# One PSUM tile of two banks and one addition for both column halves of the second product; two banks for the convolution

## The chip, the cores and the metric

The kernel runs on one core of a Trainium2 chip. The metric is the device time of one launch in microseconds. Five engines work side by side, each through its own list of instructions in order: TensorE (PE in the profile) multiplies matrices into PSUM, VectorE (DVE) and ScalarE (ACT) read PSUM and write SBUF, GpSimd (POOL) works on SBUF, and SyncE (SP) issues transfers. PSUM has eight banks; one bank holds 128 rows of 512 float32 numbers, and one product of this kernel is gathered in one bank.

## What is computed

Two branches share the normalised input, and their sum is added to the input:

```python
x = A_q                                   # (1, 2048, 576)
xn = _layernorm(x, axis=-1)
# branch A: short causal convolution of k (4 taps), times v, a long causal convolution
# of each of the 576 channels (length 2048), plus kv * ssm_D, times xn
kv = k_shift * v
y = irfft(rfft(kv_pad) * rfft(ssm_k_pad))[:S] + kv * ssm_D
# branch B: 576 -> 4608, relu, 4608 -> 576
h = jnp.maximum(jnp.einsum("bsd,df->bsf", xn, w1), 0)
return x + xn * y + jnp.einsum("bsf,fd->bsd", h, w2)
```

## The kernel before

**Precision.** Each float32 operand is split into a high and a low part, and a product is the sum of high times high, high times low and low times high. So every product is three matmuls per 128 rows of the contraction.

**Branch B, the products.** The 2048 rows are 16 tiles of 128 (t), in four blocks of four tiles (b); two blocks make a half, and the halves are worked through one after the other. The 4608 hidden columns come in 12 chunks of 384 per half (ci runs from 0 to 23), each of three tiles of 128 columns (j). `mm1` (L304) computes one hidden tile of 128 by 512 with 14 matmuls of 512 columns into one bank of the pool `ps_h` (two banks); ScalarE takes the relu into `hh` (L319) and VectorE the rest into `ll` (L320). `mm2` (L323) multiplies them with the second weights: for each row tile t and each of two halves h of the 576 output columns, nine matmuls of 288 columns (L334) into one bank of the pool `ps_o` (three banks), and then VectorE adds the bank, times the row's 1/std, to the accumulator `acc[t]` in SBUF (L337). That is 2 x 16 x 12 = 384 groups of nine matmuls and 384 additions of 128 by 288.

**Branch A, the convolution.** A generator, `conv` (L379), makes it in four stages, each a Fourier step written as matrix products of 288 columns into banks of the pool `ps_f` (three banks, `fft_psum`, L134):
- fk: 64 tiles of the kernel's transform, two matmuls each (L369), read by ScalarE (L370); VectorE splits the operands (L363).
- fx: 64 tiles of the data's transform, again L369 and L370. Here VectorE also computes the four taps (L454, L457, L458), the gate (L463) and the split (L363).
- fm: 32 groups of six tiles, three matmuls each (L533). Two tiles of k are read four times each by ScalarE (L556 to L559), two of x are read twice by ScalarE (L583, L584) and once by VectorE (L585), two of the result once by ScalarE (L573). VectorE also has L524, L563, L566 and L587.
- fo: 32 units, two for each row tile t, of two tiles, two matmuls each (L657, L658). ScalarE moves half of a tile (`low`, L659) and VectorE adds the other half to it (L660). VectorE splits the operands of a unit (`olo`, L618, after ScalarE's `ohi`, L617), multiplies the finished row tile by the gate (L625) and adds it to the accumulator, or to what the first half of the rows had stored (L632). Its loads (`zo`, `xt`, `ft`) are on SP's queue, its matrices (`wi`) and its stores for t below 8 on POOL's.

Stage four cannot start before the last group of stage three has been stored, since its loads take all of them.

**What sets the order.** The program is written with the two branches woven: after each half of an `mm1` and each half of an `mm2`, `tick` (L685) lets the generator take as many steps as its share of the work allows. When the products of the second half of the rows are in their last chunk, `rest_of_stream` (L680) writes down all that is left of the convolution ahead of the store of the row tile. This written order gives priorities only. A scheduler of the compiler then makes the list of each engine on a timeline of its own: an instruction takes its place when its operands, and a free buffer of its pool, are there by that timeline. So a pool's number of banks changes the lists of all engines. `done["acc"]` holds the last addition; the convolution's work on VectorE and ScalarE is held behind it (`here`, L373).

```python
    ps_h = ctx.enter_context(tc.tile_pool(name="ps_h", bufs=2, space=PSUM))
    ps_o = ctx.enter_context(tc.tile_pool(name="ps_o", bufs=3, space=PSUM))
    ps_f = ctx.enter_context(tc.tile_pool(name="ps_f", bufs=3, space=PSUM))
```

Of the kernel before, what the change touches and what calls it, by code (L numbers as in the profile page):

```python
# [10 lines left out]
F32 = mybir.dt.float32  # L11
F32R = mybir.dt.float32r
AF = mybir.ActivationFunctionType
OP = mybir.AluOpType
PSUM = bass.MemoryType.PSUM
DRAM = bass.MemoryType.DRAM

P = 128
# [5 lines left out]
NH = D // 2  # L24
# [83 lines left out]
def h3_ffn_kernel(ctx: ExitStack, tc, x, k, v, shift_k, ssm_k, ssm_D, w1, w2, fwd, inv, mid, out):  # L108
    nc = tc.nc
# [8 lines left out]
    xp = ctx.enter_context(tc.tile_pool(name="xp", bufs=2))  # L118
    dram = ctx.enter_context(tc.tile_pool(name="dram", bufs=1, space=DRAM))
    ps_h = ctx.enter_context(tc.tile_pool(name="ps_h", bufs=2, space=PSUM))  # L120
    ps_o = ctx.enter_context(tc.tile_pool(name="ps_o", bufs=3, space=PSUM))
    ps_f = ctx.enter_context(tc.tile_pool(name="ps_f", bufs=3, space=PSUM))

    ident = const.tile([P, P], F32, name="ident")
    make_identity(nc, ident)
# [1 line left out]
    rstd = const.tile([P, T], F32, name="rstd")  # L127
# [6 lines left out]
    def fft_psum():  # L134
        return ps_f.tile([P, 512], F32, tag="f", name="psf")

    def two(t):

        return t.rearrange("p (h n) -> p h n", h=2)


    acc = {}
# [5 lines left out]
    def move(tile_, rows, t, store=False, queues=(nc.sync, nc.sync)):  # L148
        for u in range(U):
            a, b = tile_[halves(u)[0]], rows[u, :, t]  # L150
            queues[u].dma_start(*((b, a) if store else (a, b)))
# [12 lines left out]
    def stats(t, src):  # L164
        st = xp.tile([P, 2, 6], F32, tag="bn", name=f"bn{t}", bufs=4)
        for h in range(2):
            nc.vector.bn_stats(st[:, h, :], src[:, h * NH:(h + 1) * NH])
        nc.vector.bn_aggr(mv[:, t, :], st)

    def inv_std(t0, n):  # L170

        q = xp.tile([P, 3, BT], F32, tag="q", name=f"q{t0}")[:, :, :n]
        va, h0, qu = q[:, 0, :], q[:, 1, :], q[:, 2, :]
        nc.vector.tensor_scalar(va, mv[:, t0:t0 + n, 1], EPS, None, op0=OP.add)
        nc.scalar.activation(h0, va, AF.Sqrt, scale=0.25)
        nc.vector.reciprocal(qu, h0)
        nc.vector.tensor_tensor(qu, va, qu, OP.mult)
        nc.vector.scalar_tensor_tensor(qu, qu, 0.25, h0, op0=OP.mult, op1=OP.add)
        nc.vector.reciprocal(rstd[:, t0:t0 + n], qu)
# [5 lines left out]
    def centred(dst, src, t):  # L185


        return nc.vector.tensor_scalar(dst, src, mv[:, t, 0:1], None, op0=OP.subtract)

    xT = {}  # L190
    done = {}

    def xT_tiles(b):
        hi = xp.tile([P, 4, 512], F32R, tag="xhi", name=f"xhi{b}")
        lo = xp.tile([P, 4, 512], F32R, tag="xlo", name=f"xlo{b}")
        hl = xp.tile([P, 512], F32R, tag="xhl", name=f"xhl{b}")
        xT[b] = (hi, lo, hl)

    def split_x(b, c, ps):
        hi, lo, hl = xT[b]  # L200
        if c < 4:
            nc.scalar.activation(hi[:, c, :], ps, AF.Copy)
            nc.vector.tensor_tensor(lo[:, c, :], ps, hi[:, c, :], OP.subtract)  # L203
        else:
            done["act"] = nc.scalar.activation(hl[:64, :], ps[:64, :], AF.Copy)
            done["dve"] = nc.vector.tensor_tensor(hl[64:, :], ps[:64, :], hl[:64, :],
                                                  OP.subtract)

    def first_xT(srcs):

        xT_tiles(0)
        ps = []
        for c in range(5):
            ps.append(ps_o.tile([P, 512], F32, tag="o", name=f"psx{c}") if c >= 3 else fft_psum())
        neg = xp.tile([P, BT], F32, tag="neg", name="neg", bufs=1)
        behind = None
        for t in range(BT):
            if t % 2 == 0:
                pair = xp.tile([P, 2, D], F32, tag="xn", name=f"xn{t}", bufs=BT // 2)
            xn = pair[:, t % 2, :]  # L220
            with tc.issue_after(behind.ins) if behind else nullcontext():
                stats(t, srcs[t])
                if t % 2 == 0:
                    behind = nc.vector.tensor_scalar(neg[:, t:t + 1], mv[:, t, 0:1], -1.0, None,
                                                     op0=OP.mult)
                    nc.scalar.activation(xn, srcs[t], AF.Identity, bias=neg[:, t:t + 1])
                else:
                    behind = centred(xn, srcs[t], t)
            for c in range(5):
                w = min(P, D - c * P)  # L230
                nc.tensor.transpose(ps[c][:w, t * P:(t + 1) * P], xn[:, c * P:c * P + w], ident)
        for c in range(5):
            split_x(0, c, ps[c])
        with tc.issue_after(done["dve"].ins):
            inv_std(0, BT)
# [87 lines left out]
    def mm2(ci, b, i):  # L323
        t = b * BT + i
        cols = slice(i * P, (i + 1) * P)
        for h in range(2):
            ps = ps_o.tile([P, 512], F32, tag="o", name=f"pso{ci}_{t}_{h}")
            dc = slice(h * NH, (h + 1) * NH)
            n = 0
            for j in range(FT):  # L330
                hh, ll = hid[ci, b, j]
                _, _, h2, l2 = weights[ci][j]
                for a, m in ((hh, h2), (hh, l2), (ll, h2)):
                    nc.tensor.matmul(ps[:, :NH], a[:, cols], m[:, dc],  # L334
                                     start=n == 0, stop=n == 3 * FT - 1)
                    n += 1
            done["acc"] = nc.vector.scalar_tensor_tensor(  # L337
                acc[t][:, dc], ps[:, :NH], rstd[:, t:t + 1], acc[t][:, dc],
                op0=OP.mult, op1=OP.add)
            tick(W_MM2 / 2)  # L340
        if ci % NCHUNK == NCHUNK - 1:
            if t >= HT:
                rest_of_stream()
            if t < HT:
                if t % 2:
                    nc.sync.dma_start(fin[t // 2], pairs[t - 1])
            else:
                if t >= T - 2:
                    move(acc[t], out, t, store=True)
                elif t % 2:  # L350
                    move(pairs[t - 1], out, slice(t - 1, t + 1), store=True)
# [328 lines left out]
    def rest_of_stream():  # L680
        for _ in stream:
            pass
        clock["done"] = True

    def tick(cost):  # L685

        if clock["done"] or clock["ffn"] < clock["until"]:
            clock["ffn"] += cost
            return
        clock["ffn"] += cost  # L690
        clock["conv"] += rate * cost
        if clock["conv"] < 0:
            return
        try:
            c = next(stream)
        except StopIteration:
            clock["done"] = True
            return
        if c < 0:
            clock["until"] = clock["ffn"] - c  # L700
        else:
            clock["conv"] -= c
# [11 lines left out]
    for i in range(N_WARM):  # L714
        nc.tensor.matmul(idle, warm[:, :P], warm, start=True, stop=True)
    split_w1(0, 0)
    first_xT(acc)
    for j in range(1, FT):
        split_w1(0, j)
# [9 lines left out]
    def drain(n):  # L729
        nonlocal prev  # L730
        if prev is None:
            return
        ci, b, done = prev
        for _ in range(n):
            if done < BT:
                mm2(ci, b, done)
                done += 1
        prev = (ci, b, done) if done < BT else None

    for half in range(HALVES):  # L740
        for cc in range(NCHUNK):
            ci = half * NCHUNK + cc
# [56 lines left out]
```

## Time and profile before

| | |
|---|---|
| median of three runs | 1118.28 us (1117.45 to 1119.73) |
| the profiled execution, its own time | 1114.96 us |
| span of that execution, first to last instruction | 1113.2 us |
| mean granted TensorE clock | 0.989 of full speed |
| busy share: PE, DVE, ACT, POOL | 97%, 66%, 52%, 24% |
| fk, fx, fm, fo: first to last matmul start (us) | 121 to 223, 258 to 462, 480 to 965, 983 to 1084 |

Times in the profile are microseconds from the first instruction of the span. PE is the matmul, PEld the load of its weights, which overlaps it; matmuls overlap each other too, so that their durations add up to more than the time they take. A row of a group names line, engine, operation, output and inputs, shape, count; behind the bar stand the busy time in us, the mean duration in ns, and the idle time of the engine ahead of these instructions with what ended most of it. A row of waits names who waited for whom, the sum in us, the number and the longest.

### The profile page before, as it was taken

The numbers are of one execution on the slowest core, as the hardware profiler recorded it, in microseconds if no ns is written. First come the engines' busy times: TensorE is split into PE (matmuls) and PEld (weight loads), VectorE is DVE, ScalarE is ACT, GpSimd is POOL, SyncE is SP. The second block draws the span as 40 slices with busy tenths as digits, with TensorE's granted clock in tenths as the row PEclk, the third lists the DMA queues.
The fourth block names the chain that finished last, engine by engine and source line by source line (L and its number), as shares of the span: only waits on it lengthen the run. The fifth ranks groups of instructions, "written<-read, shape, count | busy, mean of one in ns | idle before, by whom it ended". The sixth has DMA issues, their size and how long they took to land.

```text
span 1113.2 us, 17349 instructions
## 1 busy us (share of the span) xinstructions
PE 1080.5 (97%) x6534; PEld 980.5 (88%) x6534; DVE 737.3 (66%) x1215; ACT 583.5 (52%) x1180; POOL 265.4 (24%) x215
## 2 busy tenths in 40 slices
PE   8999999999999999999999999999999999998698
PEld 5889999988898988999989999999999999997587
DVE  6353876759999999358555654655555655468985
ACT  4221778713433343357566665676656666545540
POOL 3230331412412313303121131220312302214200
PEclk9999999999999999999999999999999999999699
DMA  9940464664544533426544133342342412288823
GB/s 236 175 144 1 145 192 138 191 184 140 178 145 152 180 118 130 142 75 201 175 132 132 54 122 99 96 121 64 121 123 63 131 54 90 89 247 248 232 73 86
DMA packets 112640, 150.79 MB, mean 135 GB/s; under 512 B 45229, under 2 KB 63279, under 8 KB 112556
## 3 DMA queue, kind: packets, MB, share of 16 engines
q1 hardware_dynamic: 104572, 135.98, 41.2%
q0 software_dynamic: 7824, 13.11, 4.5%
q8 instruction: 51, 0.84, 0.3%
q10 hardware_dynamic: 160, 0.59, 0.2%
q14 instruction: 33, 0.27, 0.1%
HBM read 114.26 MB, written 35.39 MB: 134 GB/s over the span
## 4 chain that ended last, share of the span: by engine, by line
PE 69%; DVE 16%; DMA 6%; issue 4%; ACT 3%; SPq 1%; POOL 1%; DVEq 0%; ACTq 0%; POOLq 0%
PE pso L334 30%; PE psh L314 29%; PE psf L533 6%; DVE e L457 4%; DVE acc L337 3%; DVE c L458 3%; DMA r<-in_w 2%; PE psf L369 2%; DVE ll L320 1%; DVE xs L363 1%; DVE c L454 1%; SPq L392 1%; DVE c L463 1%; DMA k-1_2411<-in_k 1%; POOL l L262 1%
## 5 line engine op out<-in xcount | busy, mean ns | idle before, releaser
L262 POOL TENSOR_TENSOR l<-r,h 128x640 fp32r<-128x640 f32 (+1 forms) x144 | 229.5, 1609 | 646.6 <-ACT h L297 318.7
L334 PE MATMUL pso<-h,hh 128*128 128x288 f32 x1152 | 339.0, 296 | 7.9 <-DVE acc L337 7.6
L334 PE MATMUL pso<-l,hh 128*128 128x288 f32 x1152 | 339.2, 295 | 0.0
L334 PE MATMUL pso<-h,ll 128*128 128x288 f32 x1152 | 338.9, 295 | 0.0
L337 DVE SCALAR_TENSOR_TENSOR acc<-pso,rstd,acc 128x288 f32<-128x288 f32 x384 | 193.4, 512 | 90.1 <-PE pso L334 88.3
L334 PEld LDWEIGHTS pso<-h,hh 128*128 128x128 f32 x1152 | 216.3, 188 | 17.4 <-DVE acc L337 11.3
L314 PE MATMUL psh<-xhi,h 128*128 128x512 f32 x576 | 226.7, 394 | 1.5 <-DVE ll L320 1.1
L314 PE MATMUL psh<-xlo,h 128*128 128x512 f32 x576 | 226.2, 393 | 0.0
L314 PE MATMUL psh<-xhi,l 128*128 128x512 f32 x576 | 225.6, 392 | 0.0
L334 PEld LDWEIGHTS pso<-l,hh 128*128 128x128 f32 x1152 | 216.8, 188 | 5.3
L334 PEld LDWEIGHTS pso<-h,ll 128*128 128x128 f32 x1152 | 216.7, 188 | 0.7
L320 DVE SCALAR_TENSOR_TENSOR ll<-psh,hh 128x512 fp32r<-128x512 f32 x144 | 98.6, 686 | 123.2 <-ACT hh L319 122.9
L319 ACT ACTIVATE hh<-psh 128x512 fp32r<-128x512 f32 x144 | 85.1, 593 | 141.4 <-PE psh L314 139.8
L314 PEld LDWEIGHTS psh<-xhi,l 128*128 128x128 f32 x576 | 108.5, 188 | 21.7
L314 PEld LDWEIGHTS psh<-xhi,h 128*128 128x128 f32 x576 | 108.3, 188 | 18.4 <-DVE ll L320 1.6
L314 PEld LDWEIGHTS psh<-xlo,h 128*128 128x128 f32 x576 | 108.5, 188 | 15.9 <-DVE xlo L203 0.4
L289 ACT ACTIVATE h<-r 128x640 fp32r<-128x640 f32 x72 | 52.4, 734 | 62.8 <-PE psh L314 30.4
L297 ACT ACTIVATE h<-r 128x576 fp32r<-128x576 f32 x72 | 46.9, 678 | 52.7 <-DMA r<-in_w 29.1
L585 DVE TENSOR_TENSOR k<-psf,k 128x288 f32<-128x288 f32 x64 | 29.1, 455 | 66.8 <-ACT sw L584 66.6
L583 ACT ACTIVATE sw<-psf 64x288 f32<-64x288 f32 x64 | 26.1, 408 | 88.9 <-PE psf L533 87.7
L314 PE MATMUL psh<-xhl,l 128*128 128x512 f32 x144 | 56.5, 392 | 0.0
L314 PE MATMUL psh<-xhl,h 128*128 128x512 f32 x144 | 56.2, 391 | 0.0
(104 smaller groups left out, 1414.3 us busy)
## 6 DMA issues: line engine op xcount, KB each, us to landing
r<-in_w SPq DMA_DIRECT2D x24, 864.0 KB, 6.6
r<-in_w SPq DMA_DIRECT2D x23, 768.0 KB, 5.6
zk<-zk SPq DMA_DIRECT2D x32, 288.0 KB, 2.4
zx<-zx SPq DMA_DIRECT2D x32, 288.0 KB, 2.4
ztk<-zk SPq DMA_DIRECT2D x32, 288.0 KB, 2.8
ztx<-zx SPq DMA_DIRECT2D x32, 288.0 KB, 2.8
zy<-vo SPq DMA_DIRECT2D x32, 288.0 KB, 2.2
zo<-zy SPq DMA_DIRECT2D x32, 288.0 KB, 3.5
```

The lines of the kernel that those rows point to most:

```text
L262: return nc.gpsimd.tensor_tensor(dst, src, hi, OP.subtract)
L289: nc.scalar.activation(h1, r1[:, :, cols], AF.Copy)
L297: nc.scalar.activation(h2, r2[:, j, :], AF.Copy)
L314: nc.tensor.matmul(ps, a, m, start=i == 0, stop=i == len(seq) - 1)
L319: done["act"] = nc.scalar.activation(hh, ps, AF.Relu)
L320: nc.vector.scalar_tensor_tensor(ll, ps, 0.0, hh, op0=OP.max, op1=OP.subtract)
L334: nc.tensor.matmul(ps[:, :NH], a[:, cols], m[:, dc], start=n == 0, stop=n == 3 * FT - 1)
L337: done["acc"] = nc.vector.scalar_tensor_tensor(acc[t][:, dc], ps[:, :NH], rstd[:, t:t + 1], acc[t][:, dc], op0=OP.mult, op1=OP.add)
L457: nc.vector.tensor_tensor(e, win[t - n], sk[:, n, :], OP.mult)
L458: nc.vector.tensor_tensor(sums[t], sums[t], e, OP.add)
L533: nc.tensor.matmul(ps[:, :NH], a, m[:, cols], start=n == 0, stop=n == 2)
L585: nc.vector.tensor_tensor(k1[:, cols], ps, k1[:, cols], OP.mult)
```

## The change

Both halves of the output columns of a row tile go into one tile of two banks, and VectorE adds both in one operation of 128 by 576. The pool `ps_o` has two such tiles, four banks in place of three, and `ps_f` gives one up, two in place of three. The first transposes of the input, which borrow banks from both pools, are dealt out accordingly.

```diff
-    ps_o = ctx.enter_context(tc.tile_pool(name="ps_o", bufs=3, space=PSUM))
-    ps_f = ctx.enter_context(tc.tile_pool(name="ps_f", bufs=3, space=PSUM))
+    ps_o = ctx.enter_context(tc.tile_pool(name="ps_o", bufs=2, space=PSUM))
+    ps_f = ctx.enter_context(tc.tile_pool(name="ps_f", bufs=2, space=PSUM))
...
-            ps.append(ps_o.tile([P, 512], F32, tag="o", name=f"psx{c}") if c >= 3 else fft_psum())
+            if c < 2:
+                ps.append(fft_psum())
+            else:
+                if c % 2 == 0:
+                    two_banks = ps_o.tile([P, 2, 512], F32, tag="o", name=f"psx{c}")
+                ps.append(two_banks[:, c % 2, :])
...
+        ps = ps_o.tile([P, 2, 512], F32, tag="o", name=f"pso{ci}_{t}")
         for h in range(2):
-            ps = ps_o.tile([P, 512], F32, tag="o", name=f"pso{ci}_{t}_{h}")
...
-                    nc.tensor.matmul(ps[:, :NH], a[:, cols], m[:, dc],
+                    nc.tensor.matmul(ps[:, h, :NH], a[:, cols], m[:, dc],
                                      start=n == 0, stop=n == 3 * FT - 1)
                     n += 1
-            done["acc"] = nc.vector.scalar_tensor_tensor(
-                acc[t][:, dc], ps[:, :NH], rstd[:, t:t + 1], acc[t][:, dc],
-                op0=OP.mult, op1=OP.add)
+            if h == 1:
+                done["acc"] = nc.vector.scalar_tensor_tensor(
+                    two(acc[t]), ps[:, :, :NH], rstd[:, t:t + 1], two(acc[t]),
+                    op0=OP.mult, op1=OP.add)
```

In the changed kernel the lines from `mm2` on have numbers higher by five or six: L657 is L663 there, and the addition L337 is L343.

## The prediction

> **What bounds the kernel now.** I read the page first (engines, slices, chain), then the windows by stage, then the waits in each, then the timeline of the last stage. In the windows the columns are stretch, length, busy time with instructions in brackets per engine, granted clock, DMA share, GB/s.
>
> ```profile
> span 1113.2 us, 17349 instructions
> ...
> PE 1080.5 (97%) x6534; PEld 980.5 (88%) x6534; DVE 737.3 (66%) x1215; ACT 583.5 (52%) x1180; POOL 265.4 (24%) x215
> ```
>
> ```profile
> core 0: us, PE busy (x) PEld busy (x) DVE busy (x) ACT busy (x) POOL busy (x), PEclk, DMA share, GB/s
> 258.30:461.70 203.40, 198.76 (x1205) 180.57 (x1204) 181.92 (x251) 75.69 (x148) 53.34 (x42) 1.00 0.45 139
> 479.80:964.50 484.70, 484.00 (x3012) 446.56 (x3011) 276.54 (x481) 313.41 (x673) 97.10 (x62) 1.00 0.35 107
> 983.00:1086.00 103.00, 87.86 (x485) 76.85 (x484) 91.44 (x157) 52.12 (x109) 21.91 (x33) 0.90 0.67 198
> ```
>
> The stretches are the convolution's stages two (fx), three (fm) and four (fo), by the first and last matmul of each. In fm TensorE is full (484.0 of 484.7) and VectorE has 43% free: shortening evictions there buys nothing. In fx and above all in fo VectorE is nearly full (182 of 203, 91 of 103) and TensorE waits. Two limits, then: TensorE's total of work, and VectorE in two stages. The rows of first and last starts follow (ks is stage one, fk). Since the last stage's results must precede the last products, when fo starts and how long it takes sets the end.
>
> ```profile
> L369 PE MATMUL psf<-ks,wk x128: 290/294/372, 121.0 to 222.9; 128*128 128x288 f32 x128
> L369 PEld LDWEIGHTS psf<-xs,wx x128: 187/188/191, 258.3 to 461.7; 128*128 128x128 f32 x128
> ...
> L657 PE MATMUL psf<-ohi,wi x64: 288/299/609, 983.1 to 1084.3; 128*128 128x288 f32 x64
> ...
> L658 PE MATMUL psf<-olo,wi x64: 288/294/445, 983.2 to 1084.4; 128*128 128x288 f32 x64
> ```
>
> Matmuls overlap, so their pitch, not their duration, is their cost. The chain in order of time has it:
>
> ```profile
> 84.48 3.57 PE pso L334 x27
> ...
> 94.84 3.20 PE psh L314 x14
> ...
> 1049.15 3.62 PE pso L334 x18
> ```
>
> 3.57/27 = 0.132 us for 288 columns, 3.20/14 = 0.229 us for 512. All matmuls of the program at these pitches (0.085 for a transpose, an estimate below the 288-column one) come to 1056.4 us; I call a sum of this kind TensorE work.
>
> **The change, part by part.** *The merged eviction.* 384 additions become 192 twice as wide.
>
> ```profile
> L337 DVE SCALAR_TENSOR_TENSOR acc<-pso,rstd,acc 128x288 f32<-128x288 f32 x384 | 193.4, 512 | 90.1 <-PE pso L334 88.3
> ...
> L320 DVE SCALAR_TENSOR_TENSOR ll<-psh,hh 128x512 fp32r<-128x512 f32 x144 | 98.6, 686 | 123.2 <-ACT hh L319 122.9
> ...
> L632 DVE SCALAR_TENSOR_TENSOR acc<-y,rstd,acc 128x576 f32<-128x576 f32 x8 | 6.5, 813 | 0.2
> ```
>
> The nearest row is L632: the same operation with the same scalar and accumulator on 576 columns, from SBUF, 0.813 us. Bounds: 0.74 (0.686 plus 64 columns at the same slope) and 1.02 (twice 0.512, nothing saved). I take 0.813: 193.4 - 192 x 0.813 = 37 us less VectorE work. In fm that is hidden. The first half now waits for the second before it leaves, which nobody needs sooner: each accumulator comes round once per chunk of weights.
>
> [...]
>
> *The banks.* Products had three banks and get two pairs; the convolution has two banks instead of three. Here the built order decides, in which no time stands. Matmuls that stand ahead of, within and behind the last stage on TensorE:
>
> | | ahead of the first L657: 512 / 288 columns | TensorE work ahead | within fo: 512 / 288 | behind the last L658: 512 / 288 |
> |---|---|---|---|---|
> | before | 1862 / 3932 | 957.3 | 140 / 203 | 14 / 153 |
> | after | 1940 / 4036 | 988.9 | 76 / 120 | 0 / 132 |
>
> (102 others in both; fo's own 128 not counted.) The scheduler gave convolution tiles a bank later, so convolution falls behind the products: fk's 128 matmuls spread over 132.3 us of work instead of 101.1, fm's 576 over 518.3 instead of 490.3. Only fx, which follows VectorE, is denser: 175.3 instead of 197.0. TensorE runs in order, so fo starts 78 x 0.229 + 104 x 0.132 = **31.6 us** later at least.
>
> *Stage fx.* VectorE's own work for the convolution here does not change:
>
> ```profile
> L458 DVE TENSOR_TENSOR c<-c,e 128x576 f32<-128x576 f32 x48 | 44.0, 917 | 1.1
> L457 DVE TENSOR_TENSOR e<-k,sk 128x576 f32<-128x576 f32 x42 | 43.8, 1042 | 0.3
> ...
> L363 DVE TENSOR_TENSOR xs<-c,xs 64x576 fp32r<-64x576 f32 x32 | 24.1, 753 | 5.8 <-ACT xs L362 5.0
> ...
> L463 DVE TENSOR_TENSOR c<-c,v 128x576 f32<-128x576 f32 x16 | 15.1, 943 | 0.3
> L454 DVE TENSOR_TENSOR c<-k,sk 128x576 f32<-128x576 f32 x16 | 15.0, 934 | 0.1
> ```
>
> With six more L457 on other buffers at 1.04 that is 148 us. VectorE's order from first tap to last split held 78 evictions and 29 L320 beside it, 148 + 40 + 20 = 208; now 32 and 25, 148 + 26 + 17 = 191: a factor 0.92, while TensorE work falls by 0.89. 203.4 x 0.92 = 187 against 175.3: TensorE loses 11.8 there instead of 203.4 - 197.0 = 6.4, **+5.4 us**. Lower end 0, upper +12 (evictions at 1.02 add 32 x 0.21 = 6.7).
>
> ```profile
> PEld pso L334 <- DVE acc L337: 6.8, 5, 2.1
> ```
>
> That is the wait in this stretch: products for a bank behind VectorE's queue of taps. Two pairs cover the same two groups, so it stays.
>
> *Stage fm.* Six tiles a group through two banks. TensorE work between a tile's last matmul and the next one in its bank falls, in the median, from 8.6 to 5.6 us for the L556 tiles, and is 3.7 at least. They need four ScalarE reads of about 0.41 us, 1.6 us. I take 0; the upper end is +10 us, if ScalarE's queue (313 of 485 us busy) delays a third of 32 groups by 1 us.
>
> *Stage fo.* Before, VectorE goes back to back where fo stands alone:
>
> ```profile
> 1037.50 0.75 DVE L618 TENSOR_TENSOR olo<-zo,ohi 128x576 fp32r<-128x576 f32 x1
> 1038.29 0.94 DVE L660 TENSOR_TENSOR y<-psf,low 64x288 f32<-64x288 f32 x2
> 1039.15 0.74 DVE L618 TENSOR_TENSOR olo<-zo,ohi 128x576 fp32r<-128x576 f32 x1
> 1039.82 0.80 DVE L625 SCALAR_TENSOR_TENSOR y<-xt,mv,y 128x576 f32<-128x576 f32 x1
> 1040.55 0.93 DVE L660 TENSOR_TENSOR y<-psf,low 64x288 f32<-64x288 f32 x2
> 1041.52 0.82 DVE L632 SCALAR_TENSOR_TENSOR y<-y,rstd,ft 128x576 f32<-128x576 f32 x1
> 1042.25 0.75 DVE L618 TENSOR_TENSOR olo<-zo,ohi 128x576 fp32r<-128x576 f32 x1
> ```
>
> Four tiles (one row block t) in 4.75 us. With two banks, the matmuls of tile n+2 wait for the addition of tile n, and the reads of a tile are serial:
>
> ```profile
> 1031.55 0.61 PE L657 MATMUL psf<-ohi,wi 128*128 128x288 f32 x1 [1.23 <-DVE y L660]
> 1031.96 0.44 PE L658 MATMUL psf<-olo,wi 128*128 128x288 f32 x1
> ```
>
> ```profile
> 1032.43 0.41 ACT L659 ACTIVATE low<-psf 64x288 f32<-64x288 f32 x1 [1.02 <-PE psf L658]
> ```
>
> From 1031.55 to 1032.84 is 1.29 us; VectorE has one addition and one L618, 0.45 + 0.67, in between. It lacks 0 to 0.6 us once a row block, also because an L618 waits for the L658 that frees its buffer; I take 0.4. The DMAs of a row block are two loads of zo and one each of xt, ft, wi and a store:
>
> ```profile
> zo<-zy SPq DMA_DIRECT2D x32, 288.0 KB, 3.5
> ...
> xt<-in_x SPq DMA_DIRECT2D x32, 144.0 KB, 3.9
> ...
> ft<-fin SPq DMA_DIRECT2D x8, 288.0 KB, 3.9
> out<-y POOLq DMA_DIRECT2D x16, 144.0 KB, 3.9
> wi<-in_inv POOLq DMA_DIRECT2D x16, 128.0 KB, 4.3
> ```
>
> ```profile
> 1020.00:1050.00 30.00, 19.35 (x76) 14.96 (x75) 27.24 (x48) 17.10 (x37) 8.80 (x16) 0.69 0.90 266
> ```
>
> On SP's queue the last load of weights stood among these loads and now stands ahead of them; on POOL's queue fo's wi loads and stores stand behind five of the last chunk's six splits instead of two, and those are due some 30 us before. Neither gets a price. A block carries 1.6 MB for t under 8; 266/0.90 = 296 GB/s carries that in 5.4 us, 0.25 more than 5.15. Weighted, 5.2 us a block. In the new order 78 fo matmuls, 39 tiles, stand in one run (44 before): 39/4 x 5.2 = 50.7. Ahead of it lie 5.1 us of work; behind it 34.7 of work in which fo and products alternate. The like part before (29.4 of work, from 1049.15 to 1084.4) took 35.2, so 40.5. Together **96.3** where fo took 101.3. That it is shorter is the relief of VectorE: between first and last addition stand 64 L660, 29 L618, 15 L625 and 15 L632 in both, at 0.45, 0.75, 0.80 and 0.82 us 75 us; with them stood 22 evictions and 8 L320, 92 us in all, and now stand 7 and 6, 85.
>
> [...]
>
> ```profile
> PE psf L657 <- DVE y L660: 14.9, 14, 1.5
> ```
>
> The gap repeats, but VectorE was back to back behind it, so a bank was not what lacked. By the rows alone, with the 0.4 left out, the sum is 4 us less.
>
> *The end.* Behind the last L658 stood 153 x 0.132 + 14 x 0.229 = 23.4 of work and 28.8 us passed to 1113.2, 5.4 more. Now 132 x 0.132 = 17.4 and 5.4, plus 0.3 for the wider last eviction, plus a stall: the pair that tile 9 of the last chunk needs is freed behind the last gate, sum and two evictions (0.45 + 4 x 0.8, less 0.8 of matmuls), about 3. **26.1**, 2.7 less.
>
> **The sum.** 983.1 + 31.6 + 5.4 = 1020.1 for fo's start; + 96.3 = 1116.4; + 26.1 = 1142.5. The profiled execution took 1114.96 for its span of 1113.2, so 1144.3; the median shown, 1118.28, is 3.3 above it. That execution lay below all three timed runs, so I say **1146**.
>
> **The rivals.**
> - *A faster kernel: VectorE's relief decides, not the order.* For it: VectorE is the fullest engine in fx and fo. Gain 6.4 in fx and 7 in fo: 1114.96 - 13.4 = 1102. It decides if fo starts before 983.1 + 13.4 = 996. Against it: 988.9 of work stand ahead, and what the start costs stays: 107.3 of work stand ahead of the first fk matmul, which began at 121.0, 13.7 later, so 1002 is the earliest. 0.04.
> - *Late, but lean:* fx loses no more than before, fo runs at 4.75 and alternates without loss: 983.1 + 31.6 + 5.1 + 46.3 + 36 + 23.5 = 1126, time 1128. 0.15.
> - *Two banks starve fm too:* +10 there, and fx at its upper end: 1146 + 17 = 1163. For it: distances shrink by a third; against it: none falls under 3.7 for the longest reads. 0.12.
> - *The wide operation saves nothing* (1.02 us): +6.7 in fx, +1.5 in fo, 1154. Nothing speaks for it but that no row reads two banks. 0.05.
> - *The gains just cancel the delay*, within 0.2% (about what a measurement can tell from no change): as lean, and fx and fm lose nothing at all: of the 25.8 us (983.1 - 957.3) that TensorE had lost ahead of fo, 13.7 are the start; without the other 12.1 it is 1116. 0.02.
>
> The forecast keeps 0.62, over 1134 to 1158. The range takes in the lean case and the starved one: 1126 to 1166. Faster 0.04, same 0.02, slower 0.94.
>
> **What would show it.** The first L657 (there L663) near 1020 and not under 1002; its run unbroken for some 50 us, granted clock below 0.7, TensorE waiting for the addition of L660; the merged eviction near 0.81 us; fm still full; fx's waits for the eviction near 12 us. The prediction is wrong if fo starts before 1000, or if its run takes 6 us a block or more, which would make DMA or the two banks the main cost.

## The result and the profile after

The changed kernel takes 1164.84 us (median, 1160.34 to 1165.41) against 1119.01 for the kernel before: a ratio of 1.0398 with a 95% interval of 1.0365 to 1.0432. It is slower, as forecast; the time lies 19 us above the forecast of 1146 and inside the range, close to its upper end of 1166. The profiled execution took 1164.57 us for a span of 1162.8, 49.6 us more than the 1113.2 of before.

The first lines of its page, with the slices of TensorE and of its granted clock, and the group of the merged addition (line L343; the other lines moved down by five or six: L369 is L375, L533 is L539, L617 and L618 are L623 and L624, L657 and L658 are L663 and L664, L660 is L666):

```profile
span 1162.8 us, 17276 instructions
...
PE 1099.8 (95%) x6534; PEld 993.5 (85%) x6534; DVE 706.7 (61%) x1023; ACT 589.8 (51%) x1180; POOL 259.8 (22%) x215
...
PE   8999999999899999999999999999999999974777
...
PEclk9999999999999999999999999999999999995779
...
L343 DVE SCALAR_TENSOR_TENSOR acc<-pso,rstd,acc 128x576 f32<-128x576 f32 x192 | 156.1, 814 | 101.2 <-PE pso L339 99.6
```

VectorE did get its relief (737.3 to 706.7 us busy), and the last four slices show the price: TensorE at 0.4 to 0.7 and its clock at 0.5 to 0.9. The starts of fx, fm and fo follow; of fm it is the matmuls that end last, with their row of the kernel before ahead of them:

```profile
L533 PE MATMUL psf<-yh,m_sb x128: 290/294/401, 495.0 to 973.8; 128*128 128x288 f32 x128
```

```profile
L539 PE MATMUL psf<-yh,m_sb x128: 291/295/402, 506.6 to 1017.8; 128*128 128x288 f32 x128
...
L375 PE MATMUL psf<-xs,wx x128: 290/294/442, 278.7 to 468.8; 128*128 128x288 f32 x128
...
L663 PE MATMUL psf<-ohi,wi x64: 292/442/610, 1030.7 to 1138.6; 128*128 128x288 f32 x64
...
L664 PE MATMUL psf<-olo,wi x64: 292/442/445, 1030.8 to 1138.8; 128*128 128x288 f32 x64
```

So in the table of the profile before, fm's last matmul starts at 973.8 us, not at 965. The waits of the weight loads over the whole span (sum, times, longest, in us), one row of before and then those of after:

```profile
PEld psf L657 <- DVE y L660: 19.8, 18, 1.7
```

```profile
PEld psf L663 <- DVE y L666: 43.2, 26, 2.3
PEld pso L339 <- DVE acc L343: 5.7, 8, 2.2
PEld psf L375 <- ACT zx L376: 3.5, 2, 2.9
...
PEld psf L539 <- ACT k L565: 3.2, 4, 1.0
PEld psf L375 <- DVE xs L369: 2.8, 2, 1.8
...
PEld psf L539 <- DVE k L591: 2.6, 5, 1.2
```

The wait of fo's matmuls for the addition that frees their bank grew from 19.8 to 43.2 us; waits of the convolution inside fx and fm are new and small. Two windows of fo follow, the first with its run of matmuls without products, which goes from 1035.7 to 1089.1 us, the second with the part in which fo and products alternate (columns as in the windows of before):

```profile
1030.00:1092.00 62.00, 33.54 (x118) 25.84 (x117) 48.29 (x83) 29.15 (x61) 14.22 (x26) 0.59 0.84 253
1092.00:1139.00 47.00, 40.23 (x213) 35.61 (x212) 32.59 (x54) 18.55 (x38) 3.02 (x4) 0.85 0.25 68
```

And one tile pair of that run in the timeline (start, duration, engine, in brackets the idle time ahead and its releaser):

```profile
1064.27 0.94 DVE L666 TENSOR_TENSOR y<-psf,low 64x288 f32<-64x288 f32 x2
1064.77 0.61 PE L663 MATMUL psf<-ohi,wi 128*128 128x288 f32 x1 [1.76 <-DVE y L666]
1065.17 0.44 PE L664 MATMUL psf<-olo,wi 128*128 128x288 f32 x1
1065.41 0.68 ACT L623 ACTIVATE ohi<-zo 128x576 fp32r<-128x576 f32 x1 [1.68 <-PE psf L663]
1065.41 0.45 PE L663 MATMUL psf<-ohi,wi 128*128 128x288 f32 x1
1065.67 0.44 PE L664 MATMUL psf<-olo,wi 128*128 128x288 f32 x1
1066.12 0.83 ACT L665 ACTIVATE low<-psf 64x288 f32<-64x288 f32 x2
1066.13 0.76 DVE L624 TENSOR_TENSOR olo<-zo,ohi 128x576 fp32r<-128x576 f32 x1 [0.92 <-ACT ohi L623]
1066.92 0.94 DVE L666 TENSOR_TENSOR y<-psf,low 64x288 f32<-64x288 f32 x2
...
1071.89 0.76 DVE L624 TENSOR_TENSOR olo<-zo,ohi 128x576 fp32r<-128x576 f32 x1 [0.93 <-ACT ohi L623]
```

An addition frees a bank, a matmul takes it, that matmul's end frees the operand buffer that `ohi` waits for, `olo` waits for `ohi`, and the next addition stands behind `olo` on VectorE: a loop, with the matmuls at 0.44 to 0.61 us instead of 0.29. A row block takes 1071.89 - 1066.13 = 5.76 us, where VectorE alone set 4.75 before.

Behind that run the alternating part took 49.7 us (1089.1 to 1138.8) for 34.7 us of work. Two more stretches of fo without products stand in it, of 8 and 12 matmuls. They took 4.4 and 6.8 us for 1.1 and 1.6 of work, and the 18 products behind each ran at the lower clock at first, 4.3 and 4.1 us for 2.4 (the clock's records say 0.50 from 1112.4 to 1119.2 us and from 1126.0 to 1132.9). The two waits of the first stretch, and the first product behind it:

```profile
1110.79 0.40 PE L663 MATMUL psf<-ohi,wi 128*128 128x288 f32 x1 [0.96 <-DVE y L666]
...
1113.88 0.61 PE L663 MATMUL psf<-ohi,wi 128*128 128x288 f32 x1 [2.08 <-DVE y L666]
...
1115.22 0.61 PE L339 MATMUL pso<-h,hh 128*128 128x288 f32 x1
```

**One measure for all that follows.** Every kernel here does the same 1056.4 us of TensorE work (counted with the prediction's pitches; the 0.085 us for a transpose was the author's estimate, where the trace of before has the transposes of L258 0.109 us apart in the median, and it is the same in every kernel's sum), so span less 1056.4 is what TensorE lost: to waits, to the lower clock, and at both ends. It is split at fo's first matmul: lost ahead of it (its start less the work ahead of it in the built order) and lost from there to the end. Before: 25.8 and 31.0. After: 41.9 and 64.5 (fo from 1030.7 to its last matmul, an L664, at 1138.8, so 108.1 us long, with 24.0 behind it).

### The profile page after: what moved, and what is told of

Read it like the earlier page. It is cut to its first block, busy times and chain, and to the rows that moved or that the text cites. A ratio compares the mean times of both kernels' runs of the same rounds, so it can differ in the third digit from the quotient of the medians.

```text
span 1162.8 us, 17276 instructions
## 1 busy us (share of the span) xinstructions
PE 1099.8 (95%) x6534; PEld 993.5 (85%) x6534; DVE 706.7 (61%) x1023; ACT 589.8 (51%) x1180; POOL 259.8 (22%) x215
## 5 line engine op out<-in xcount | busy, mean ns | idle before, releaser
L267 POOL TENSOR_TENSOR l<-r,h 128x640 fp32r<-128x640 f32 (+1 forms) x144 | 224.1, 1566 | 659.6 <-ACT h L302 483.2
L339 PE MATMUL pso<-h,hh 128*128 128x288 f32 x1152 | 343.4, 298 | 4.8 <-DVE acc L343 3.5
L339 PEld LDWEIGHTS pso<-h,hh 128*128 128x128 f32 x1152 | 219.2, 190 | 12.0 <-DVE acc L343 5.7
L339 PEld LDWEIGHTS pso<-l,hh 128*128 128x128 f32 x1152 | 219.3, 190 | 4.9
L339 PEld LDWEIGHTS pso<-h,ll 128*128 128x128 f32 x1152 | 219.1, 190 | 1.1
L343 DVE SCALAR_TENSOR_TENSOR acc<-pso,rstd,acc 128x576 f32<-128x576 f32 x192 | 156.1, 814 | 101.2 <-PE pso L339 99.6
L369 DVE TENSOR_TENSOR ks<-kt,ks 64x288 fp32r<-64x288 f32 x64 | 50.7, 792 | 34.7 <-ACT ks L368 33.2
L591 DVE TENSOR_TENSOR k<-psf,k 128x288 f32<-128x288 f32 x64 | 29.1, 456 | 67.0 <-ACT sw L590 60.2
L663 PE MATMUL psf<-ohi,wi 128*128 128x288 f32 x64 | 28.2, 445 | 35.2 <-DVE y L666 35.2
```

Source lines behind the costliest of these rows:

```text
L267: return nc.gpsimd.tensor_tensor(dst, src, hi, OP.subtract)
L339: nc.tensor.matmul(ps[:, h, :NH], a[:, cols], m[:, dc], start=n == 0, stop=n == 3 * FT - 1)
L343: done["acc"] = nc.vector.scalar_tensor_tensor(two(acc[t]), ps[:, :, :NH], rstd[:, t:t + 1], two(acc[t]), op0=OP.mult, op1=OP.add)
L369: nc.vector.tensor_tensor(dst[other], src[own], dst[own], OP.subtract)
L591: nc.vector.tensor_tensor(k1[:, cols], ps, k1[:, cols], OP.mult)
L663: nc.tensor.matmul(ps[:, :NH], w[:, u, :], hi[:, cols], start=True, stop=False)
```

## The experiments

**The banks alone, and the additions alone.** Kernel e1_banks is the kernel before with the convolution's third bank taken away and nothing else:

```diff
-    ps_f = ctx.enter_context(tc.tile_pool(name="ps_f", bufs=3, space=PSUM))
+    ps_f = ctx.enter_context(tc.tile_pool(name="ps_f", bufs=2, space=PSUM))
...
-            ps.append(ps_o.tile([P, 512], F32, tag="o", name=f"psx{c}") if c >= 3 else fft_psum())
+            ps.append(ps_o.tile([P, 512], F32, tag="o", name=f"psx{c}") if c >= 2 else fft_psum())
```

> The kernel before with two banks in place of three for the convolution and nothing else: products keep three single banks and their 384 additions of 288 columns; one bank lies idle. Theory A (the convolution's third bank carries the loss): the built order already has 989 us of TensorE work ahead of the last stage's first matmul, as in the changed kernel; that matmul comes at 1020 to 1035 us, a row block of the last stage takes 5.75 us instead of 4.75, and the time is 1155 to 1180. Theory B (the pairs and the wide addition carry it): 1115 to 1125.

1168.41 us, ratio 1.0456 (1.0423 to 1.0489). The whole loss is there without any pair and without any merged addition, so taking the convolution's third bank is enough for it. The same loop stands in fo:

```profile
1065.62 0.76 DVE L618 TENSOR_TENSOR olo<-zo,ohi 128x576 fp32r<-128x576 f32 x1 [0.92 <-ACT ohi L617]
...
1071.36 0.76 DVE L618 TENSOR_TENSOR olo<-zo,ohi 128x576 fp32r<-128x576 f32 x1 [0.92 <-ACT ohi L617]
```

Kernel e3_split_add keeps the changed kernel's pairs, but adds each half by itself:

```diff
-            if h == 1:
-                done["acc"] = nc.vector.scalar_tensor_tensor(
-                    two(acc[t]), ps[:, :, :NH], rstd[:, t:t + 1], two(acc[t]),
-                    op0=OP.mult, op1=OP.add)
+            done["acc"] = nc.vector.scalar_tensor_tensor(
+                acc[t][:, dc], ps[:, h, :NH], rstd[:, t:t + 1], acc[t][:, dc],
+                op0=OP.mult, op1=OP.add)
```

> The changed kernel with the merging undone: each half of a pair is added by its own operation as soon as its nine matmuls are done; the banks stay two pairs and two. Theory A: 1150 to 1175, near the 1164.8 of the changed kernel, since the convolution's banks are the same (968 us of work, not 976, end stage three, so a little less is possible). Theory B: most of the loss goes, under 1135.

1186.69 us, ratio 1.062 (1.0585 to 1.0655), above what any theory had named. Products wait for the additions, 20 times and up to 5.6 us:

```profile
PEld pso L339 <- DVE acc L342: 19.6, 20, 5.6
```

With the pairs as they are, merging gains 1186.7 - 1164.8 = 22 us (the built order moved too, its longest run of fo from 66 to 78). So nothing here makes the merged addition a part of the loss.

**A bank given back.** Kernel e2_pairs_h1 takes a bank from the first product instead of the convolution:

```diff
-    ps_h = ctx.enter_context(tc.tile_pool(name="ps_h", bufs=2, space=PSUM))
+    ps_h = ctx.enter_context(tc.tile_pool(name="ps_h", bufs=1, space=PSUM))
...
-    ps_f = ctx.enter_context(tc.tile_pool(name="ps_f", bufs=2, space=PSUM))
+    ps_f = ctx.enter_context(tc.tile_pool(name="ps_f", bufs=3, space=PSUM))
```

> The changed kernel with the third bank given back to the convolution; the bank is taken from the first product, which then has one instead of two. The merged addition stays. Theory A: 926 us of TensorE work ahead of the last stage, its first matmul at 945 to 965 us, row blocks of 4.75 us or slower only where products stand between, the time 1085 to 1120. Theory B: the pairs stay, so the time stays over 1145. If the first product suffers from its single bank, TensorE waits for the relu's readers (L320's group) by more than 10 us and the time is over 1120.

1145.45 us, ratio 1.0245 (1.0217 to 1.0274): better than the change, worse than before. From fo's start on it lost only 19.6 us, but ahead of it 66.8, 41 more than the kernel before. A part of that is `mm1` waiting for its one bank, 15.1 us; what makes up the rest was not separated:

```profile
PEld psh L319 <- DVE ll L325: 15.1, 18, 3.7
```

The run of fo had gone from its order (longest: 10 matmuls), but two things changed at once, so it settles little alone.

**Operand buffers.** Kernel e4_hi4 gives the split operands of fo a fourth buffer, against the loop's step from matmul to `ohi`:

```diff
-                    hi = fp.tile([P, D], F32R, tag="hi", name=f"ohi{t}_{u}", bufs=3)
-                    lo = fp.tile([P, D], F32R, tag="lo", name=f"olo{t}_{u}", bufs=3)
+                    hi = fp.tile([P, D], F32R, tag="hi", name=f"ohi{t}_{u}", bufs=4)
+                    lo = fp.tile([P, D], F32R, tag="lo", name=f"olo{t}_{u}", bufs=4)
```

> The changed kernel with four buffers instead of three for the split operands of the last stage (hi and lo); the order of TensorE hardly moves (988.8 us of work ahead of the stage in both). If the operand buffers carry the delay in a row block (VectorE waits 0.92 us for the split that waits for the matmul that frees its buffer), a block falls from 5.75 to 4.8 to 5.2 us and the time by 6 to 12 us. If the two banks do it by themselves, the block stays within 0.2 us of 5.75 and the time within 3 us of the changed kernel.

1163.73 us, ratio 1.0405 (1.0377 to 1.0433): no change. The block is 5.75 us still, and `olo` still waits 0.92 us for `ohi`:

```profile
1068.16 0.76 DVE L624 TENSOR_TENSOR olo<-zo,ohi 128x576 fp32r<-128x576 f32 x1 [0.93 <-ACT ohi L623]
...
1073.91 0.76 DVE L624 TENSOR_TENSOR olo<-zo,ohi 128x576 fp32r<-128x576 f32 x1 [0.92 <-ACT ohi L623]
```

The scheduler moved `ohi` forward by as much as the buffer allowed: in the run each `ohi` starts four matmuls, one unit, earlier in fo's list than in the changed kernel. So it waits for another matmul of the same loop.

**Is it lateness?** The convolution can be written earlier by one constant, in both kernels (e5_share85 the changed one, e6_b_share85 the one before):

```diff
-SHARE = 0.95
+SHARE = 0.85
```

> The changed kernel, with one constant changed: the convolution is spread over 0.85 of the products' work instead of 0.95, so that it is written earlier. In the built order fo now lies between 878.7 and 949.7 us of TensorE work, where it lay from 988.9 on in the changed kernel and from 957.3 on in the kernel before; banks are as in the changed kernel. Theory A (lateness in the order is what costs): fo is out of the way by about 1010 us, and products alone stand behind it, about 107 us of work; the end comes near 1118 us or under, a gain of 40 us or more on the changed kernel. Theory B (two banks cost where they run): fo's blocks still take 5.75 us, fx and fm still lose 26 us to waits, and the time stays at 1140 us or more.

> The kernel before, with the same constant changed from 0.95 to 0.85. In the built order fo lies between 881.1 and 931.8 us of TensorE work, 76 us ahead of its place in the kernel before. It is the control for the same constant in the changed kernel: if lateness costs, it should gain too, but less, since its fo ended only 29 us before the end: both theories expect 1100 to 1120 us. Theory A expects the changed kernel with this constant within 15 us of it; theory B 25 us or more slower.

1212.72 us for the changed kernel, ratio 1.0843 (1.0818 to 1.0868), and 1166.61 for the one before, 1.0427 (1.04 to 1.0453). With fo 110 us of work earlier the changed kernel loses another 48 us: lateness in the order isn't what costs, and the theory that it is falls. What the earlier convolution has instead is length without products. The changed kernel's windows of the end of fm, and of fo:

```profile
900.00:973.00 73.00, 44.85 (x177) 34.62 (x176) 29.62 (x46) 49.27 (x110) 5.94 (x4) 0.69 0.19 64
973.00:981.00 8.00, 0.90 (x5) 0.58 (x4) 0.73 (x1) 2.14 (x4) 1.61 (x3) 0.50 0.53 174
981.00:1102.00 121.00, 91.36 (x469) 79.05 (x470) 89.94 (x149) 53.93 (x110) 25.31 (x35) 0.74 0.61 181
```

In its built order the longest stretch of matmuls of one stage with no product between them is 102 in fm and 82 in fo (in the changed kernel 6 and 78, in the kernel before 9 and 44), and the loss moved with it: 60 us more ahead of fo, 10 less from there on. The new theory: the loss is the runs that the scheduler's order makes of the convolution, and two banks cost because with them its order has longer runs.

**The same banks in another order.** Both kernels with the scheduler's simulated timeline off, e8_b_nosim the kernel before and e8_a_nosim the changed one:

```diff
-    with tile.TileContext(nc, schedule_with_timeline_sim=True) as tc:
+    with tile.TileContext(nc, schedule_with_timeline_sim=False) as tc:
```

> The kernel before (three single banks for products, three for the convolution), with the scheduler's own reordering switched off: every engine gets its instructions in the order in which the source writes them. In that built order fm lies between 457.8 and 856.7 us of TensorE work and fo between 872.3 and 1007.5, whatever the number of banks. This is the base for the next kernel; its own time is not what the theories part on. Both expect TensorE's work of about 1056 us plus the start's 13 and some stalls, 1090 to 1180 us: fo is no longer last but spread, while TensorE meets waits that the scheduler would have filled.

> The changed kernel (two pairs, merged addition, two convolution banks), with the same reordering switched off, so that the stages stand at the same places on TensorE as in the other kernel without reordering. Theory A (the built order carries the loss: fo's matmuls stand 31.6 us of work later, and only because the scheduler was told of fewer banks): with the order held equal the two kernels lie within 10 us of each other. Theory B (the banks carry it while the kernel runs: each chain through two banks waits longer, wherever it stands): the changed kernel is slower by 15 us or more. Rival from the additions alone (VectorE's relief of 37 us): the changed kernel is faster by over 3 us.

1118.6 us for the kernel before, ratio 1.0005 (0.9989 to 1.0021): its time is the same, though it now loses 51.9 us ahead of fo and 8.2 from there on, where it was 25.8 and 31.0. **1103.17 us for the changed kernel, ratio 0.986 (0.9834 to 0.9886)**, 62 us less than as changed, and faster than the kernel before. Same banks, same merged addition, same work; only the order differs. In it fo's matmuls stand two at a time between products. The changed kernel's fo there, then the waits of its matmuls, first as changed (1030 to 1140 us), then in this order (900 to 1060 us):

```profile
L663 PE MATMUL psf<-ohi,wi x64: 292/295/402, 908.4 to 1047.9; 128*128 128x288 f32 x64
```

```profile
PE psf L663 <- DVE y L666: 35.2, 23, 2.1
```

```profile
PE psf L663 <- DVE y L666: 1.6, 2, 0.9
PE psf L664 <- DVE olo L624: 1.2, 2, 1.0
```

Two banks are enough for fo when products stand between its tiles: 35.2 us of this wait became 1.6 (these rows are of the matmuls; the 43.2 above are of their weight loads). Theory A (within 10 us of each other) and theory B (15 us slower) both failed; the rival from VectorE's relief, over 3 us faster, had the sign right, and the next run shows that the relief is half of it.

**What the change is worth in that order.** Kernel e11_o4_nosim is e8_b_nosim with the eight banks divided as in the change, four for products and two for the convolution, but single, with 384 additions:

```diff
-    ps_o = ctx.enter_context(tc.tile_pool(name="ps_o", bufs=3, space=PSUM))
-    ps_f = ctx.enter_context(tc.tile_pool(name="ps_f", bufs=3, space=PSUM))
+    ps_o = ctx.enter_context(tc.tile_pool(name="ps_o", bufs=4, space=PSUM))
+    ps_f = ctx.enter_context(tc.tile_pool(name="ps_f", bufs=2, space=PSUM))
```

> The kernel before without the scheduler's reordering, its eight banks divided as in the changed kernel but not paired: four single banks for products, two for the convolution, 384 additions. Between the two kernels without reordering lay 15.4 us (1118.6 to 1103.2), and the wait of products for an addition fell from 15.3 to 1.3 us. Theory M (the merged addition gives it, as VectorE's queue is what products waited for): 1115 us or more, the wait near 15 us. Theory P (the fourth bank of products gives it): 1107 us or less, the wait under 4 us.

1110.92 us, ratio 0.9926 (0.9898 to 0.9953), between the theories: the fourth bank and the merging in pairs give about half of the 15.4 us each, 7.7 and 7.7. The fourth bank of products takes the wait for an addition out of fx, and the convolution, with a bank less, pays a part of it back. The row of e8_b_nosim, then those of e11_o4_nosim, for 250 to 470 us:

```profile
PEld pso L334 <- DVE acc L337: 12.4, 6, 3.3
```

```profile
PEld psf L369 <- ACT zx L370: 4.9, 3, 2.6
PEld pso L334 <- DVE acc L337: 0.3, 1, 0.3
```

Its last fx matmul starts at 459.1 instead of 466.0 us. The merged addition then gives its half in fm: from first to last fm matmul 423.3 us (477.1 to 900.4) became 416.0 (476.7 to 892.7).

**A run put in by hand.** If runs are the cause, one made in the good order must cost what a run costs. 39 tiles of fo are written with no pause for products, and the pace is made up behind them; no stage starts later (e12_a_bunch from e8_a_nosim, e13_b_bunch from e8_b_nosim):

```diff
+            owed = 0
             for n, (t, u) in enumerate(units):
...
-                    yield W_FO
+                    owed += W_FO
+                    if not 8 <= 2 * n + h < 46:
+                        yield owed
+                        owed = 0
```

> The changed kernel without reordering (1103.2 us), in which 39 of fo's tiles are written one behind the other with no products between, and products alone follow until the convolution's pace is made up. Nothing starts later than it did, and banks, work and every other stage stay. In the built order the longest run of fo's matmuls is 56 where it was 2; 28 tiles are 7 row blocks. Theory C (what costs is that the scheduler's order puts tiles of two banks in runs with no products between): 7 blocks of 5.75 us take 40 us, of which 7.4 are TensorE's work, so 33 us are added: 1136 us, 1125 to 1150, with a granted clock near 0.6 there. Theory L (lateness or the banks alone): no change, 1103 within 5 us.

> The kernel before without reordering (1118.6 us), with the same 39 tiles of fo written in one go; the longest run in the built order is 59 matmuls. Three banks here. Theory C: about 7.4 blocks of 4.75 us take 35 us, of which 7.8 are TensorE's work: 27 us are added, 1146 us, 1135 to 1158; a block is 1.0 us shorter than with two banks, so that the run costs some 6 us less than in the changed kernel. Theory L: no change, 1118.6 within 5 us.

1133.08 us with two banks, ratio 1.0137 (1.009 to 1.0183), 29.9 more than without the run (33 expected); 1148.98 with three, ratio 1.0277 (1.0239 to 1.0314), 30.4 more (27 expected). The runs themselves, of 56 and 59 matmuls, took 35.3 and 36.5 us for 7.4 and 7.8 of work. The windows of e12_a_bunch in the run and behind it:

```profile
940.00:980.00 40.00, 28.80 (x79) 18.96 (x79) 34.70 (x60) 19.47 (x41) 8.82 (x17) 0.53 0.82 237
980.00:1000.00 20.00, 20.00 (x120) 18.14 (x119) 6.16 (x8) 5.24 (x9) 8.96 (x6) 1.00 0.31 94
```

So runs cost, with two banks or three, and products between the tiles cure it. One part of the expectation fell: a block here takes 4.75 us at its best with **two** banks, 5.0 on the average of the run, and with three it was no less (5.0). So the 33 us came near with a wrong block. The same operand of e12_a_bunch, one block apart:

```profile
951.17 0.74 DVE L624 TENSOR_TENSOR olo<-zo,ohi 128x576 fp32r<-128x576 f32 x1
951.84 0.80 DVE L631 SCALAR_TENSOR_TENSOR y<-xt,mv,y 128x576 f32<-128x576 f32 x1
...
954.22 0.81 DVE L638 SCALAR_TENSOR_TENSOR y<-y,rstd,ft 128x576 f32<-128x576 f32 x1
...
955.93 0.74 DVE L624 TENSOR_TENSOR olo<-zo,ohi 128x576 fp32r<-128x576 f32 x1
...
960.68 0.74 DVE L624 TENSOR_TENSOR olo<-zo,ohi 128x576 fp32r<-128x576 f32 x1
```

`olo` waits for nothing there, and VectorE is busy for 34.70 of 40 us where the changed kernel left it idle for 0.9 us in each block. In the changed kernel's run L631 and L638 stand side by side behind one pair of additions and nothing stands behind the other, where `olo` waits; here each pair has one of the two behind it. So two banks as such do not set 5.75 us; that this place of the two operations does is read from the rows, and no run moved them alone.

**A try for more.** Kernel e14_a_share97 is e8_a_nosim with the convolution spread further:

```diff
-SHARE = 0.95
+SHARE = 0.97
```

> The changed kernel without reordering, the convolution spread over 0.97 of the products' work instead of 0.95. A try at a faster kernel: fx, where VectorE is busy 181 of 204 us, gets 8.8 us of TensorE work more to cover it, and fo ends 18 us of work later, 31 us of work before the end. Theory C: 1097 to 1104 us, a gain if fx's waits shrink by more than the end's grow. Theory L (lateness costs by itself): 1115 us or more.

1102.39 us, ratio 0.9862 (0.9825 to 0.9899): the same as e8_a_nosim within what can be told. fo stands 13.5 us of work later at no cost that can be seen, once more against lateness.

All profiled spans by the one measure (longest run: matmuls of fo with no product between them in the built order):

| kernel | longest run in fo | lost ahead of fo | lost from fo on |
|---|---|---|---|
| before | 44 | 25.8 | 31.0 |
| after | 78 | 41.9 | 64.5 |
| e1_banks | 78 | 45.0 | 66.4 |
| e3_split_add | 66 | 72.1 | 57.9 |
| e2_pairs_h1 | 10 | 66.8 | 19.6 |
| e4_hi4 | 78 | 42.4 | 65.6 |
| e5_share85 | 82 | 102.3 | 54.7 |
| e6_b_share85 | 85 | 63.5 | 47.1 |
| e8_b_nosim | 2 | 51.9 | 8.2 |
| e8_a_nosim | 2 | 36.1 | 9.7 |
| e11_o4_nosim | 2 | 43.7 | 8.9 |
| e12_a_bunch | 56 | 34.8 | 40.2 |
| e13_b_bunch | 59 | 51.9 | 38.6 |
| e14_a_share97 | 2 | 40.5 | 5.7 |

The last column goes with the run, from 6 to 10 us without one to 65 at 78 matmuls, though not by length alone: e5_share85 and e6_b_share85 lose 55 and 47 us with 82 and 85. With the timeline off, the list isn't quite the written one either: 39 tiles in one go became a run of 28.

## Why the prediction was right or wrong

It was right in sign and in the main cause, fo in a run of 78 matmuls with products moved ahead of it, and too low in size: it forecast 29 us more of span, and 50 came. That the range held is in part luck: its upper end, 1 us above the measured time, stood for a rival with other losses. By its own steps, in us:

| step | forecast | measured |
|---|---|---|
| fo behind more products | +31.6 | the order has it, as counted |
| more lost in fx | +5.4 | +8.4 |
| more lost in fm | 0 | +7.6 |
| fo's start | 1020.1 | 1030.7 |
| fo's length | 96.3 | 108.1 |
| of it the run of 78 | 50.7 | 53.4 |
| of it the alternating part | 40.5 | 49.7 |
| the end behind fo | 26.1 | 24.0 |
| span | 1142.5 | 1162.8 |

- **The order.** The 31.6 us were right as a shift of fo's start, but read alone they mislead. The same 31.6 us of products are missing within fo (25.6) and behind it (6.0), so the shift by itself costs nothing. In lost time the forecast was 5.4 in fx, 20.7 in fo (46.2 instead of 25.5) and 3.3 at the end, together 29.4; measured were 8.4, 7.6 in fm, 32.5 and 1.2, together 49.7. That lateness does not pay is what e5_share85 and e14_a_share97 then showed.
- **fx, near in size, with another wait.** fx took 190.1 us where 187 was forecast. But "two pairs cover the same two groups, so it stays" failed. The prediction looked for about 12 us of waits for the addition there; the wait of products for it fell, from 6.8 to 3.1 us between 250 and 470 us. In its place the convolution waits, 3.5 us for the ScalarE reading that frees its bank (`zx`).
- **The merged addition.** 0.813 us forecast, 0.814 measured as the length of a row: an addition that reads two banks lasts as long as the same shape from SBUF. But rows of VectorE overlap, so an operation's length is not what it costs the engine's list. Two lines of before, then two of after, show it:

```profile
262.29 0.50 DVE L337 SCALAR_TENSOR_TENSOR acc<-pso,rstd,acc 128x288 f32<-128x288 f32 x1
262.72 0.74 DVE L458 TENSOR_TENSOR c<-c,e 128x576 f32<-128x576 f32 x1
```

```profile
1100.30 0.82 DVE L343 SCALAR_TENSOR_TENSOR acc<-pso,rstd,acc 128x576 f32<-128x576 f32 x1
1101.03 0.68 DVE L325 SCALAR_TENSOR_TENSOR ll<-psh,hh 128x512 fp32r<-128x512 f32 x1
```

Where the next operation starts ahead of an addition's end, it starts 0.428 us behind the start of a single one and 0.728 behind that of a merged one (medians of 184 and 59). So by these distances merging frees 384 x 0.428 - 192 x 0.728 = 25 us of VectorE's time, not the 37 of the lengths. "In fm that is hidden" was not shown: in the other order the merged addition gave 7.7 us, most of it in fm, and with pairs but single additions (e3_split_add, whose order differs too) fm lost 31.7 us, against 11.4 in the changed kernel.
- **fm, a term put at nothing.** "I take 0" rested on the distance between two tiles in one bank, 5.6 us in the median. The trace has waits of fm for reads by ScalarE (L565, 3.2 us) and VectorE (L591, 2.6 us), short and new; they sum to less than 7.6 us, and what the rest is was not separated. The prediction also ended fm too early, at 964.5 us: with the matmuls of `yh` it took 493.9 us for 490.2 of work before, and 529.5 for 518.2 after. That TensorE was full there before stands.
- **fo, the step that cost most.** The run of 78 had the right mechanism. Its block settled at 5.75 us instead of 5.2, since the 0.4 for two banks saw matmul, reading and addition, but not that the loop goes on through `ohi` and `olo`; as the tiles at its ends took less, the run came out at 53.4 instead of 50.7. The larger miss, 9.2 us, is the part behind it. "The like part before took 35.2, so 40.5" carried 5.8 us of loss over, and 15.0 were lost: the two further stretches without products, and the products behind each stretch at the lower clock. DMA, which the prediction would have blamed from 6 us a block, was not it: e12_a_bunch moves 237 GB/s at 4.75 us a block.
- **The rivals.** "A faster kernel" by VectorE's relief lost here, since fo started at 1030.7 and not below 996; in the other order the change is faster by 15.4 us where this rival had 13.4, but that is luck: half of it is the fourth bank of products, and the relief's half lies in fm, where the rival had none. "Late, but lean" and "the gains just cancel the delay" fell with fo's start and its block. "Two banks starve fm too" came nearest in time (1163), with 12 us in fx and 10 in fm where 8.4 and 7.6 were measured, but left fo at its forecast, where 12 of the missing 20 us lie. "The wide operation saves nothing" fell with 0.814.
- **A gap that repeats.** The prediction read the 14.9 us in 14 waits of fo's matmuls for the addition as VectorE's queue, not as the lack of a bank. After the change the same wait was 35.2 us in 23; with two banks and products between the tiles (e8_a_nosim) it was 1.6 us in 2, so two banks as such do not make it.

**What stays open.** Why the scheduler's timeline makes runs of the convolution, and longer ones with two banks, is not in any trace. How much of a run's loss is the halved clock and how much the waits was not separated. The 16 us that the change lost ahead of fo, in fx and fm, were followed to their waits alone; in the other order the same two banks lose less there than three (36.1 and 51.9). The order without the timeline loses more ahead of fo with three banks than the one with it (51.9 and 25.8); an order that takes the better of both was not tried.

## What to carry to other kernels

A pool's number of banks is also an input of the scheduler: when a change of banks moves the time, compare the built orders and count how long a chain stands without independent work between its links, before blaming the banks. Time gained or lost by the engine that is full is best kept as lost time, span less its fixed work; a shift of a stage's start is no cost as long as the work it passes is not missing beside it. To judge a change by itself, run it in a second order as well: here the same edit was 4.0% slower in one and, against the same kernel, 1.4% faster in the other.

## What the runs showed of the hardware

The granted clock was low where the convolution stood alone and TensorE had gaps: 0.53 between 940 and 980 us of e12_a_bunch, with TensorE busy for 28.80 of 40 us, and 1.00 in the 20 us behind, when products were back and it was busy for all of them; a matmul of 288 columns took up to 0.61 us in e12_a_bunch's fo instead of 0.29. The clock records in the traces of before and after hold two values alone, 1.00 and 0.50. Those of 0.50 sum to 26.0 us before, 20.5 of them from 1031.2 to 1051.7, and to 83.1 after the change, 51.2 of them from 1040.7 to 1091.9, where the run of fo went from 1035.7 to 1089.1. The waits alone do not tell a run's price, since the work in it slows down too: the products behind that run start 0.24 us apart up to 1091.7 us and 0.13 apart from 1091.9 on. The lowest window seen is 0.50, between 973 and 981 us of e5_share85, with TensorE busy for 0.90 of 8 us.

Rows of VectorE overlap: a merged addition lasts 0.814 us, and the next operation, where it started ahead of the addition's end, started 0.728 us behind its start (median of 59). So what an operation costs VectorE is read here from start to start.
